# Sixteen attention steps take over the first conversion of the weights in an attention and Mish feed-forward kernel

## The chip, the cores and the metric

The kernel runs on one core of one Trainium2 chip. The metric is the device time of one execution in microseconds (us); the kernel before has a median of 900.63 us over three runs (898.88 to 900.71). A difference of 0.2%, about 1.8 us, is about what a measurement of this kernel can tell from no change.

## The reference

Attention with queries pooled in pairs (four batches, eight heads, 1152 keys of 64), and behind it a feed-forward layer with a Mish activation over 2304 rows of 512. All inputs are float32.

```python
q_pool = q.reshape(B, H, S // 2, 2, D).mean(axis=3)
scores = scale * np.matmul(q_pool, k.transpose(0, 1, 3, 2))
scores = scores - np.max(scores, axis=-1, keepdims=True)
attn = np.exp(scores)
attn = attn / (np.sum(attn, axis=-1, keepdims=True) + 1e-09)
attn_out = np.matmul(attn, v)
x = attn_out.transpose(0, 2, 1, 3).reshape(B * S_pooled, H * D)
h = x @ w_in
out = (h * np.tanh(np.log1p(np.exp(h)))) @ w_out
```

## The kernel before

The program has two parts. The first is attention in 32 **steps**: a pair of heads has two steps, one for each half of its queries. In a step the keys go by in nine chunks of 128. For chunk c of step i the kernel has these functions:

- `QK(i, c)` (L204, TensorE): four matrix products into a score tile `s` in PSUM. There are only two such tiles, so chunk c + 2 starts when chunk c's tile has been read.
- `CP(i, c)` (L214, ScalarE) copies the tile into `T3`, and `MX(i, c)` (L221, VectorE) takes it into the running maximum `rmax`, for c = 1 to 8. The two read one tile one after the other. "The sixth maximum" is `MX(i, 6)`, on the tile that the order of instructions calls `s_6`, and "the seventh" is `MX(i, 7)`.
- `MT`, `TMAX`, `MB` (L230 TensorE, L235 VectorE, L244 TensorE) turn the maxima into one per query, spread over all partitions as the tile `Mb`.
- `SUB` (L252, VectorE), `EXP` (L256, ScalarE), `PV` (L273, TensorE) subtract, exponentiate and multiply with the values, in four groups of chunks. `EXP` of group 1 comes ahead of that of group 0; `PV(i, 0)` waits for group 0.
- `ADD(i, 0)` to `ADD(i, 4)` (L262, L264, L266, GpSimd) sum the exponentials. `ADD(i, 0)` reads four chunks of `T3`, from SBUF, once group 0 is exponentiated. The next use of the same half of `T3`, `CP(i + 2, 0)`, waits for it.
- `QP` (L125, GpSimd) pools the queries of a coming pair, `TG` and `TGc` (L145, L148 TensorE; L156 to L161 ScalarE) transpose its keys and queries and copy them out of PSUM.

The second part is the feed-forward layer, on the weights split into a high and a low half. A 128-row piece of a weight matrix is made by `load_w(n)` (one or four DMAs on SyncE's queue) and six conversion stages `conv(n, 0)` to `conv(n, 5)`:

- stage 0: ScalarE, a scaled copy to the tile `wt` (L436);
- stages 1, 2 and 3: VectorE, all in int32 and 128x512: a shift of `wt` (L440), and two operations that take the raw weights and `wt` together, both from SBUF (L442, L446). Stage 3 also calls `load_w(n + 2)`;
- stage 4: ScalarE, the high half `wh` (L455);
- stage 5: GpSimd, the low half `wl`, `wt` minus `wh` (L458).

Pieces 0 to 3 are converted in the attention part, all others in the feed-forward part.

The order on every engine is written by hand. Each call has a due time in units of a step: `STEP` and `PAIR` give it relative to a step, so `(MX, 6, 0.245)` stands for i + 0.245 in step i. All calls are sorted by due time, and each engine runs its instructions strictly in that order. `CONV0` lists the due times of the six stages of pieces 0 to 3. Due time 4.245 is `MX(4, 6)`, 4.464 is `MX(4, 7)`, and 4.267 is `ADD(3, 0)`.

`first()` runs ahead of the sorted plan: it loads the first pair, keeps TensorE busy with 52 transposes that nothing reads, and prepares the first keys and queries.

Of the kernel before, what the change touches and what calls it, by code (L numbers as in the profile page):

```python
# [22 lines left out]
def tile_pooled_attention_then_mish_ffn(ctx: ExitStack, tc: tile.TileContext, q, k, v, moe_w_in, moe_w_out, out):  # L23
# [42 lines left out]
    if True:  # L66
# [22 lines left out]
        def load_q(p):  # L89
            if p >= B * NP:  # L90
                return
            b, hp = divmod(p, NP)
            qn = pre.tile([QB, 2, 6, P], F32, tag="qn", name=f"qn{p}")
            for j in range(2):
                sp.dma_start(out=qn[:, j], in_=q[b, 2 * hp + j].rearrange("(n p r) d -> p n (r d)", p=QB, r=2))
            raw[p] = [None, qn]

        def load_k(p):
            if p >= B * NP:
                return  # L100
            b, hp = divmod(p, NP)
            kn = pre.tile([P, NC, 2, D], F32, tag="kn", name=f"kn{p}")
            for j in range(2):
                o = kn[:, :, j] if p else T3[:, 1, j].rearrange("p a b -> p (a b)").rearrange("p (c d) -> p c d", d=D)
                sp.dma_start(out=o, in_=k[b, 2 * hp + j].rearrange("(p c) d -> p c d", c=NC))
                if p == 0:
                    (act.copy if j else dve.tensor_copy)(kn[:, :, j], o)
            raw[p][0] = kn
# [3 lines left out]
        def load_v(p):  # L112
            if p >= B * NP:
                return
            b, hp = divmod(p, NP)
            vs[p] = p2.tile([P, 2, NC, D], F32, tag="vn", name=f"vn{p}")
            sp.dma_start(out=vs[p], in_=v[b, 2 * hp:2 * hp + 2].rearrange("h (p c) d -> p h c d", c=NC))
# [3 lines left out]
        def QP(p):  # L121

            x = raw[p][1].rearrange("p j n m -> p n j m")
            qp = pre.tile([QB, 6, 2, D], F32, tag="qp", name=f"qp{p}")
            (pool if p else dve).tensor_tensor(qp, x[:, :, :, 0:D], x[:, :, :, D:2 * D], ALU.add)  # L125
            prepped[p] = qp.rearrange("p n j d -> p n (j d)")

        def qk_tiles(p):
            qT = pqk.tile([P, SQ], F32, tag="qT", name=f"qT{p}")
            kT = pqk.tile([P, NC, P], F32, tag="kT", name=f"kT{p}")  # L130
            qk[p] = (kT, qT)
# [3 lines left out]
        def kblock(p, c):  # L135
            return raw[p][0][:, c].rearrange("p j d -> p (j d)")
# [26 lines left out]
        def first():  # L163

            load_q(0)
            load_k(0)
            load_w(0)
            load_w(1)
            QP(0)
            if NWARM:  # L170
                x = ps1.tile([P, 4, P], F32R, tag="x", name="warm")
                for n in range(NWARM):
                    pe.transpose(x[:, n % 4], identr, identr)  # L173
            qk_tiles(0)
            kT, qT = qk[0]
            t = psS.tile([P, 2, 512], F32, tag="S", name="xq0")
            for n in range(6):
                pe.transpose(t[:, n // 3, n % 3 * QB:(n % 3 + 1) * QB], prepped[0][:, n], ident[0:QB, 0:QB])
            act.copy(qT[:, 0:HQ], t[:, 0, 0:HQ])
            dve.tensor_copy(qT[:, HQ:SQ], t[:, 1, 0:HQ])  # L180
            x = psS.tile([P, 8, P], F32, tag="S", name="xk0")
            for n in range(8):
                pe.transpose(x[:, n], kblock(0, n), ident)
            act.copy(kT[:, 0:4], x[:, 0:4])
            dve.tensor_copy(kT[:, 4:8], x[:, 4:8])
            x = ps1.tile([P, 512], F32, tag="x", name="xk0_2")
            pe.transpose(x[:, 0:P], kblock(0, 8), ident)
            act.copy(kT[:, 8], x[:, 0:P])
            load_q(1)
            load_k(1)  # L190

        rmaxs, Mbs, pvs, accs = {}, {}, {}, {}

# [222 lines left out]
        def load_w(n):  # L416
            if n >= len(pieces):
                return
            f, io = pieces[n]
            if io:  # L420
                r = wraw_p.tile([P, DM, 2], I32, tag="raw", name=f"ro{f}")
                sp.dma_start(out=r, in_=wo32[f * P:(f + 1) * P])
            else:
                r = wraw_p.tile([P, NKC, P, 2], I32, tag="raw", name=f"ri{f}")
                for c in range(NKC):
                    sp.dma_start(out=r[:, c], in_=wi32[:, c, f * P:(f + 1) * P])
                r = r.rearrange("p c m two -> p (c m) two")
            wraw[n] = r
# [90 lines left out]
        def O_(bu, f):  # L519
            gh, gl = gs.pop((bu, f))  # L520
            wh, wl = ws[f, 1]
            first, last = f in F0, f + 1 in F0
            if first:
                os_[bu] = o_tiles(bu)
            for t in range(UT // P):
                a, b = gh[:, t * P:(t + 1) * P], gl[:, t * P:(t + 1) * P]
                for m, (x, y) in enumerate(((a, wh), (a, wl), (b, wh))):
                    pe.matmul(os_[bu][t], x, y, start=(first and m == 0), stop=(last and m == 2))  # L528
# [67 lines left out]
            plan += [(i + t, fn, i, *a) for i in range(NS) if i < NS - 1 or fn not in GONE]  # L596
        plan += [(NS + t, fn, NS - 1) for fn, t in LAST.items()]
        for fn, *a, t in PAIR:
            first_p = 2 if fn in (load_q, load_k) else 0 if fn is load_v else 1
            plan += [(2 * p + t, fn, p, *a) for p in range(first_p, B * NP)]  # L600
        CONV0 = [
            (-0.26, -0.17, -0.16, -0.13, -0.05, -0.04),
            (-0.02, 0.07, 0.09, 0.10, 0.20, 0.21),
            (0.35, 0.40, 0.47, 0.49, 0.55, 0.56),
            (0.60, 0.66, 0.67, 0.78, 0.85, 0.86),
        ]
        for n, t in enumerate(CONV0):
            plan += [(t[m], conv, n, m) for m in range(6)]
# [4 lines left out]
        for g in range(len(seq) + 8):  # L613
            t = NS + T3F + DT * (g - 3)
            for fn, *a in FLOW:
                if fn in (split, convs):
                    plan.append((t, fn, g, *a))
                elif 0 <= g - a[0] < len(seq):
# [3 lines left out]
                    else:  # L622
                        plan.append((t, *e))
        first()
        plan.sort(key=lambda e: e[0])
        for _, fn, *a in plan:
# [32 lines left out]
```

## Time and profile before

| | us |
|---|---|
| median of three runs | 900.63 |
| the three runs | 900.71, 900.63, 898.88 |
| the profiled execution | 898.73 |
| its span in the profile | 897.0 |
| VectorE busy in the span | 591.7 |
| ScalarE busy in the span | 539.7 |
| GpSimd busy in the span | 454.8 |
| TensorE busy in the span, by modelled ends | 872.7 |

The span is the time from the first to the last instruction, 1.7 us less than the execution's time. A row of the timeline gives start, duration, engine, line, operation, result and operands, shapes, and in brackets the idle time of the engine ahead of it and what ended it. PE is TensorE's products, PEld its weight loads, DVE is VectorE, ACT ScalarE, POOL GpSimd. A row of the page's costliest groups gives the total busy time and the mean of one in ns. A row of busy time by stretches gives the stretch and its length, then the busy time (and instructions) of PE, PEld, DVE, ACT and POOL, then the granted clock as a share of full speed, the DMA share and GB/s.

### The profile page before, as it was taken

Reading aid. Unit: us, or ns where it says so; the run is one execution under the profiler, and the core shown is the slowest. Engines: PE = TensorE matmul, PEld = TensorE weight load, DVE = VectorE, ACT = ScalarE, POOL = GpSimd, SP = SyncE. Lnnn points to the kernel's source line nnn. Section 1 sums busy time; section 2 is a strip of 40 time slices with the busy share of each in tenths; the row PEclk is TensorE's granted clock in tenths of the full one; section 3 lists DMA queues with packets and bytes.
Section 4 is the critical chain, followed back from the end, with each engine's and each line's share of the span. In section 5 each row is a group of like instructions: output and inputs, shape, how many; then the busy total and the mean of one; then the engine's idle time right before and its main releaser. Section 6 shows DMA issues by size and latency. Waiting matters only on the chain.

```text
span 897.0 us, 14672 instructions
## 1 busy us (share of the span) xinstructions
PE 872.7 (97%) x5668; PEld 590.1 (66%) x5668; DVE 591.7 (66%) x812; ACT 539.7 (60%) x997; POOL 454.8 (51%) x268
## 2 busy tenths in 40 slices
PE   6899999999999999999998999999999999999997
PEld 4444444444444444444445899999999999999996
DVE  4898988998889888988897733443555334432222
ACT  4788888888888888888886753333333333322221
POOL 1489888988889888998889520111111011100000
PEclk9799999999999999999999999999999999999999
DMA  6412223132321323132200210111122011001112
GB/s 176 129 40 68 75 59 80 27 80 55 80 59 48 80 54 80 27 80 53 74 2 1 71 49 24 48 48 47 50 71 71 24 48 48 24 1 48 48 48 70
DMA packets 75109, 50.74 MB, mean 57 GB/s; under 512 B 37408, under 2 KB 68640, under 8 KB 75040
## 3 DMA queue, kind: packets, MB, share of 16 engines
q1 hardware_dynamic: 75040, 49.82, 19.8%
q8 instruction: 44, 0.72, 0.3%
q14 instruction: 25, 0.20, 0.1%
HBM read 45.09 MB, written 4.72 MB: 56 GB/s over the span
## 4 chain that ended last, share of the span: by engine, by line
PE 84%; ACT 7%; POOL 6%; DVE 2%; issue 1%; DVEq 0%; POOLq 0%; ACTq 0%
PE h L495 23%; PE s L204 16%; PE pv L273 13%; PE o L528 11%; POOL acc L262 5%; ACT T L214 3%; ACT T L256 3%; PE mt L230 2%; PE xt L145 2%; PE Mb L244 2%; PE xt L148 1%; DVE T L252 1%; PE Sb L295 1%; PE warm L173 1%; POOL xl L477 0%
## 5 line engine op out<-in xcount | busy, mean ns | idle before, releaser
L204 PE MATMUL s<-qT,kT 64*128 64x288 f32 x1152 | 211.9, 454 | 12.8 <-DVE rmax L221 6.3
L510 DVE TENSOR_TENSOR gl<-g,gh 128x256 fp32r<-128x256 f32 x144 | 66.3, 461 | 230.9 <-ACT gh L505 200.2
L500 ACT ACTIVATE g<-h 128x256 f32<-128x256 f32 x144 | 55.6, 386 | 249.2 <-PE h L495 249.1
L214 ACT COPY T<-s 128x576 f32<-128x576 f32 x288 | 181.4, 641 | 36.9 <-DVE rmax L221 16.1
L252 DVE TENSOR_TENSOR T<-T,Mb 128x1152 f32<-128x1152 f32 (+1 forms) x128 | 191.3, 1496 | 11.1 <-PE Mb L244 11.0
L273 PE MATMUL pv<-T,vn 128*64 128x288 f32 x1152 | 194.3, 428 | 1.2 <-ACT T L256 0.5
L221 DVE TENSOR_TENSOR rmax<-s,rmax 128x576 f32<-128x576 f32 x224 | 169.0, 754 | 37.3 <-ACT T L214 30.6
L458 POOL TENSOR_TENSOR wl<-wt,wh 128x512 fp32r<-128x512 f32 x32 | 41.8, 1308 | 256.2 <-ACT wh L455 212.3
L256 ACT ACTIVATE T<-T 128x1152 f32<-128x1152 f32 (+1 forms) x128 | 166.0, 1297 | 6.9 <-DVE T L252 4.9
L264 POOL TENSOR_TENSOR acc<-acc,T 128x1152 f32<-128x1152 f32 x64 | 168.7, 2636 | 2.7 <-ACT T L256 0.2
L204 PEld LDWEIGHTS s<-qT,kT 64*128 64x128 f32 x1152 | 89.5, 189 | 117.7 <-issue 40.8
L495 PE MATMUL h<-xh,wh 128*128 128x256 f32 x576 | 162.0, 281 | 0.0
L495 PE MATMUL h<-xh,wl 128*128 128x256 f32 x576 | 161.8, 281 | 0.0
L495 PE MATMUL h<-xl,wh 128*128 128x256 f32 x576 | 161.6, 281 | 0.0
L273 PEld LDWEIGHTS pv<-T,vn 128*64 128x64 f32 x1152 | 63.7, 136 | 88.6 <-issue 58.9
L495 PEld LDWEIGHTS h<-xh,wh 128*128 128x128 f32 x576 | 108.7, 189 | 8.1 <-issue 2.2
L495 PEld LDWEIGHTS h<-xl,wh 128*128 128x128 f32 x576 | 108.9, 189 | 6.0
L495 PEld LDWEIGHTS h<-xh,wl 128*128 128x128 f32 x576 | 109.2, 190 | 0.0
L262 POOL TENSOR_TENSOR acc<-T 128x1152 f32<-128x1152 f32 x32 | 84.7, 2645 | 44.6 <-ACT T L256 43.7
L528 PE MATMUL o<-wh,gh 128*128 128x512 f32 x146 | 57.7, 395 | 0.0
L528 PE MATMUL o<-wl,gh 128*128 128x512 f32 x146 | 57.5, 394 | 0.0
L528 PE MATMUL o<-wh,gl 128*128 128x512 f32 x146 | 57.3, 392 | 0.0
(380 smaller groups left out, 1094.2 us busy)
## 6 DMA issues: line engine op xcount, KB each, us to landing
qn<-in_q_dram SPq DMA_DIRECT2D x32, 288.0 KB, 3.8
vn<-in_v_dram SPq DMA_DIRECT2D x16, 576.0 KB, 4.9
kn<-in_k_dram SPq DMA_DIRECT2D x30, 288.0 KB, 4.1
ri<-in_moe_w_in_dram SPq DMA_DIRECT2D x64, 128.0 KB, 2.2
ro<-in_moe_w_out_dram SPq DMA_DIRECT2D x16, 512.0 KB, 3.5
out_dram<-xT SPq DMA_DIRECT2D x18, 256.0 KB, 2.6
T<-in_k_dram SPq DMA_DIRECT2D x2, 288.0 KB, 4.8
```

The lines of the kernel that those rows point to most:

```text
L204: pe.matmul(s[:, j, 0:HQ], kT[64 * j:64 * j + 64, c], qT[64 * j:64 * j + 64, hf * HQ:(hf + 1) * HQ], start=True, stop=True,)
L214: act.copy(T3[:, i % 2, c], ss[i, c])
L221: dve.tensor_tensor(r, ss[i, c], T3[:, i % 2, 0] if c == 1 else r, ALU.max)
L252: dve.tensor_tensor(x, x, Mbs[i][:, :, 0:HQ].unsqueeze(1).to_broadcast([P, w, 2, HQ]), ALU.subtract)
L256: act.activation(x, x, AF.Exp, scale=0.0625)
L262: pool.tensor_tensor(accs[i], t[:, 0:2], t[:, 2:4], ALU.add)
L264: pool.tensor_tensor(accs[i], accs[i], t[:, 2 * n + 2:2 * n + 4], ALU.add)
L273: pe.matmul(pvs[i][64 * j:64 * j + 64, 0:HQ], vn[:, j, c, :], T3[:, i % 2, c, j], start=(c == 0), stop=(c == NC - 1),)
L495: pe.matmul(h[:, 0:UT], a, b, start=(m == 0), stop=(m == len(seq) - 1))
L500: act.activation(g, hs[bu, f], AF.Mish)
L510: dve.tensor_tensor(gl, ch.pop((bu, f)), f32(gs[bu, f][0]), ALU.subtract)
L528: pe.matmul(os_[bu][t], x, y, start=(first and m == 0), stop=(last and m == 2))
```

## The change

`CONV0` is replaced. Before, the 24 stages have due times from -0.26 to 0.86, in the first step. Now stage m of piece n is due in step 4n + 2 and later: stage 0 at 4n + 2.73, the three VectorE stages at 4n + 3.30, 4n + 4.30 and 4n + 5.30, stage 4 at 4n + 5.73 and stage 5 at 4n + 6.955. The four pieces so reach from 2.73 to 18.955. In `first()` the loads of pieces 0 and 1 move behind the loads of the second pair, and the first load of the values, `load_v(0)`, moves ahead of them. The loads of pieces 2 and 3 hang on stage 3 of pieces 0 and 1 and go with them.

```diff
             load_q(0)
             load_k(0)
-            load_w(0)
-            load_w(1)
             QP(0)
...
             load_q(1)
             load_k(1)
+            load_v(0)
+            load_w(0)
+            load_w(1)
...
-            first_p = 2 if fn in (load_q, load_k) else 0 if fn is load_v else 1
+            first_p = 2 if fn in (load_q, load_k) else 1
...
         CONV0 = [
-            (-0.26, -0.17, -0.16, -0.13, -0.05, -0.04),
-            (-0.02, 0.07, 0.09, 0.10, 0.20, 0.21),
-            (0.35, 0.40, 0.47, 0.49, 0.55, 0.56),
-            (0.60, 0.66, 0.67, 0.78, 0.85, 0.86),
+            tuple(4 * n + 2 + a for a in (0.73, 1.30, 2.30, 3.30, 3.73, 4.955)) for n in range(4)
         ]
```

In the order of VectorE's instructions the first step looked so before (`rmax0` is step 0's maximum, `s0_4` its chunk 4; `wt0`, `wt1` and `ri0`, `ri1` belong to pieces 0 and 1):

```order
L221 TENSOR_TENSOR rmax0_216<-s0_3_223,rmax0_216 128x576
L440 TENSOR_SCALAR wt0_227<-wt0_227 128x512
L442 SCALAR_TENSOR_TENSOR wt0_227<-ri0_113,wt0_227 128x512
L221 TENSOR_TENSOR rmax0_216<-s0_4_230,rmax0_216 128x576
L446 SCALAR_TENSOR_TENSOR wt0_227<-ri0_113,wt0_227 128x512
L221 TENSOR_TENSOR rmax0_216<-s0_5_238,rmax0_216 128x576
L440 TENSOR_SCALAR wt1_250<-wt1_250 128x512
L442 SCALAR_TENSOR_TENSOR wt1_250<-ri1_118,wt1_250 128x512
L446 SCALAR_TENSOR_TENSOR wt1_250<-ri1_118,wt1_250 128x512
L221 TENSOR_TENSOR rmax0_216<-s0_6_253,rmax0_216 128x576
```

Of the change, the same place on VectorE (lines from 164 on are numbered a little differently):

```order
L222 TENSOR_TENSOR rmax0_218<-s0_3_225,rmax0_218 128x576
L222 TENSOR_TENSOR rmax0_218<-s0_4_230,rmax0_218 128x576
L222 TENSOR_TENSOR rmax0_218<-s0_5_236,rmax0_218 128x576
L222 TENSOR_TENSOR rmax0_218<-s0_6_242,rmax0_218 128x576
L222 TENSOR_TENSOR rmax0_218<-s0_7_247,rmax0_218 128x576
L222 TENSOR_TENSOR rmax0_218<-s0_8_257,rmax0_218 128x576
L222 TENSOR_TENSOR rmax1_268<-s1_1_262,T3_98 128x576
```

All conversion stages are gone from between the maxima of step 0, and from the same stretch of ScalarE and GpSimd.

Further on, step 4 on VectorE before, around its sixth and seventh maximum:

```order
L221 TENSOR_TENSOR rmax4_650<-s4_5_700,rmax4_650 128x576
L252 TENSOR_TENSOR T3_98<-T3_98,Mb3_684 128x1152
L221 TENSOR_TENSOR rmax4_650<-s4_6_712,rmax4_650 128x576
L221 TENSOR_TENSOR rmax4_650<-s4_7_725,rmax4_650 128x576
L252 TENSOR_TENSOR T3_98<-T3_98,Mb3_684 128x1728
L221 TENSOR_TENSOR rmax4_650<-s4_8_753,rmax4_650 128x576
```

The same place of VectorE in the change:

```order
L222 TENSOR_TENSOR rmax4_613<-s4_5_663,rmax4_613 128x576
L253 TENSOR_TENSOR T3_98<-T3_98,Mb3_647 128x1152
L222 TENSOR_TENSOR rmax4_613<-s4_6_675,rmax4_613 128x576
L443 SCALAR_TENSOR_TENSOR wt0_510<-ri0_201,wt0_510 128x512
L222 TENSOR_TENSOR rmax4_613<-s4_7_688,rmax4_613 128x576
L253 TENSOR_TENSOR T3_98<-T3_98,Mb3_647 128x1728
L222 TENSOR_TENSOR rmax4_613<-s4_8_717,rmax4_613 128x576
```

Stage 2 of piece 0 now stands between the two maxima of step 4. Stage 1 stands at the same place in step 3 and stage 3 in step 5; pieces 1, 2 and 3 follow four, eight and twelve steps later.

## Rows read from the trace of the kernel before

**Rows 1.** The page's costliest groups: the copy of a score tile, and stage 5.

```profile
L214 ACT COPY T<-s 128x576 f32<-128x576 f32 x288 | 181.4, 641 | 36.9 <-DVE rmax L221 16.1
...
L458 POOL TENSOR_TENSOR wl<-wt,wh 128x512 fp32r<-128x512 f32 x32 | 41.8, 1308 | 256.2 <-ACT wh L455 212.3
```

**Rows 2.** The chain that ended last, 90 to 130 us, shares by line.

```profile
by line: PE s L204 42.2%; PE pv L273 39.1%; PE xt L145 5.7%; PE mt L230 4.1%; PE Sb L295 3.6%; PE Mb L244 3.2%; PE xt L148 2.2%; issue 0.3%
```

**Rows 3.** Timeline of POOL: `ADD(i, 0)` of steps 0, 1, 4 and 5.

```profile
38.69 2.64 POOL L262 TENSOR_TENSOR acc<-T 128x1152 f32<-128x1152 f32 x1 [2.88 <-ACT T L256]
...
52.32 2.65 POOL L262 TENSOR_TENSOR acc<-T 128x1152 f32<-128x1152 f32 x1 [0.70 <-ACT T L256]
...
95.80 2.64 POOL L262 TENSOR_TENSOR acc<-T 128x1152 f32<-128x1152 f32 x1 [3.22 <-ACT T L256]
...
109.43 2.65 POOL L262 TENSOR_TENSOR acc<-T 128x1152 f32<-128x1152 f32 x1 [0.16 <-ACT T L256]
```

**Rows 4.** Timeline, step 0 from its fifth chunk to `PV(0, 0)`.

```profile
15.78 0.76 PE L204 MATMUL s<-qT,kT 64*128 64x288 f32 x4 [0.67 <-ACT T L214]
...
28.89 1.33 PE L230 MATMUL mt<-identr,rmax 128*128 128x128 f32 x5
...
31.91 0.80 PE L244 MATMUL Mb<-identr,m 128*128 128x128 f32 x6
...
33.84 0.62 ACT L455 CAST wh<-wt 128x512 fp32r<-128x512 f32 x1
...
34.81 1.19 ACT L256 ACTIVATE T<-T 128x1152 f32<-128x1152 f32 x1
...
38.67 1.19 PE L273 MATMUL pv<-T,vn 128*64 128x288 f32 x8 [0.54 <-ACT T L256]
```

**Rows 5.** Busy time and granted clock (PEclk) of three stretches of the start.

```profile
14.40:17.80 3.40, 2.15 (x12) 0.86 (x12) 3.04 (x5) 1.77 (x4) 0.64 (x1) 1.00 0.06 12
17.80:21.20 3.40, 0.83 (x6) 0.30 (x4) 1.73 (x3) 2.14 (x4) 1.27 (x1) 1.00 0.42 154
21.20:31.40 10.20, 7.39 (x25) 3.62 (x25) 8.41 (x14) 5.37 (x9) 2.55 (x2) 0.50 0.56 167
```

**Rows 6.** Timeline, step 6: `MX(6, 7)`, and the weight loads of `QK(6, 8)`.

```profile
110.55 0.76 DVE L221 TENSOR_TENSOR rmax<-s,rmax 128x576 f32<-128x576 f32 x1 [0.29 <-ACT T L214]
...
111.36 0.30 PEld L204 LDWEIGHTS s<-qT,kT 64*128 64x128 f32 x4 [0.23 <-DVE rmax L221]
```

**Rows 7.** Timeline: `MX(5, 6)`, `MX(5, 7)`, `CP(6, 0)` and `CP(5, 8)`, `TGc` of queries.

```profile
94.91 0.75 DVE L221 TENSOR_TENSOR rmax<-s,rmax 128x576 f32<-128x576 f32 x1
...
96.92 0.76 DVE L221 TENSOR_TENSOR rmax<-s,rmax 128x576 f32<-128x576 f32 x1 [1.25 <-ACT T L214]
...
98.47 1.18 ACT L214 COPY T<-s 128x576 f32<-128x576 f32 x2 [0.19 <-POOL acc L262]
...
103.71 0.40 ACT L161 COPY qT<-xt 128x288 f32<-128x288 f32 x1 [0.90 <-PE xt L148]
```

**Rows 8.** Timeline, VectorE and GpSimd together on operands in SBUF.

```profile
488.77 2.63 POOL L264 TENSOR_TENSOR acc<-acc,T 128x1152 f32<-128x1152 f32 x1
...
489.31 2.37 DVE L510 TENSOR_TENSOR gl<-g,gh 128x256 fp32r<-128x256 f32 x1 [3.61 <-ACT gh L505]
...
494.50 1.81 POOL L477 TENSOR_TENSOR xl<-xT,xh 128x256 fp32r<-128x256 f32 x2
...
495.74 1.11 DVE L442 SCALAR_TENSOR_TENSOR wt<-ri,wt 128x512 int32<-128x512 int32 x1
...
499.99 0.69 DVE L442 SCALAR_TENSOR_TENSOR wt<-ro,wt 128x512 int32<-128x512 int32 x1
...
499.99 1.29 POOL L477 TENSOR_TENSOR xl<-xT,xh 128x256 fp32r<-128x256 f32 x1 [3.68 <-ACT xh L476]
...
506.98 0.42 DVE L440 TENSOR_SCALAR wt<-wt 128x512 int32<-128x512 int32 x1
...
293.19 0.73 POOL L477 TENSOR_TENSOR xl<-xT,xh 128x256 fp32r<-128x256 f32 x1 [0.77 <-ACT xh L476]
```

## The prediction

> **What bounds the kernel now.** I read the chain that ended last first. In the attention steps it runs on TensorE alone: products of scores and values, transposes, 0.3% for anything else [rows 2]. VectorE, ScalarE and GpSimd have idle time there, but only where the row of the one behind it is not a product: whatever makes a score product start later lengthens the step. Next I read where the steps settle. `ADD(0, 0)` and `ADD(1, 0)` start 13.63 us apart, and so do those of steps 4 and 5 [rows 3]. So the attention part keeps its pace from `PV(0, 0)`, at 38.67 [rows 4], and all ahead of it is a ramp. The change does two things: it shortens the ramp, and it puts work between two maxima of twelve steps that run at TensorE's pace. The end is the ramp's gain against what those twelve steps lose.
>
> **The ramp.** In step 0 a score tile goes through product (0.76), copy (0.64) and maximum (0.76), one after the other, and the tile two chunks on waits for the maximum [rows 1, 4, 6]. A hand-over takes 0.05: `MX(6, 7)` ends at 110.55 + 0.76 = 111.31 and the weights that waited for it are loaded at 111.36 [rows 6]. One link is so 0.76 + 0.64 + 0.76 + 3 x 0.05 = 2.31. `QK(0, 5)` starts at 15.78 [rows 4], which is ahead of any place where a conversion stage has cost something. From it three links, chunks 5, 7 and 8 (chunk 6 and the next step's first chunk go by in between), end `MX(0, 8)` at 15.78 + 6.93 = 22.71. `MT` stands behind one more product, 0.05 + 0.76 later: 23.5. Before, it starts at 28.89 [rows 4]: **5.4** gained.
>
> From `MT` to `MB` it took 3.02 (28.89 to 31.91), and `MT` 1.33 of it, at a granted clock of 0.50, the lower level of 1.2 GHz; `MB` already ran at full clock, 0.80 for six transposes [rows 4, 5]. At full clock `MT` takes about half, 0.6 less, and the score product and four key transposes between the two are also cut; a third VectorE stage of about 0.7 stood in the way as well. I take **1.1**, with 0 (the clock falls as before) and 1.5 as bounds. From `MB` to `EXP` of group 1 ScalarE did a `wh` of 0.62 first [rows 4], and the copies behind it had their data: **0.5**. From there to `PV(0, 0)`, 3.86, nothing is taken out. In sum 7.0: `PV(0, 0)` at 31.7. Bounds 5.4 and 7.5.
>
> The fall of the clock came behind a stretch with 0.83 of 3.40 us busy on TensorE; the stretch ahead of that had 2.15, and no fall behind it [rows 5]. In the new ramp the stretch from 17.8 to 21.2 holds three score products of 0.76, about 2.3 us. I therefore expect no fall.
>
> The moved loads cost nothing: keys and queries of the first pair stand ahead of the weights in the queue before and after, and the weights have until step 2. What covers the later loads is a step or more: `load_w(2)` now stands in SyncE's queue ahead of `load_k(4)` and waits for stage 3 in step 5, but those keys are transposed more than a step later. If that cover were gone, each of two such waits would cost the few microseconds of one landing.
>
> **The steps: ScalarE and GpSimd.** Stage 4 (0.62) goes ahead of a copy of queries that waits 0.90 for TensorE [rows 4, 7]; stage 0, of the same size, stands in the other kind of step ahead of the copy of keys, which waits for the same engine. Both go at nothing. Stage 5 (1.31 [rows 1]) stands between the last addition of an odd step and `ADD` of the even one, where GpSimd waits 3.22 [rows 3]: nothing. Without those waits each would cost its own length, four times.
>
> **The steps: VectorE.** Between the two maxima VectorE idles 1.25 us in odd steps [rows 7] and 0.29 in even ones [rows 6]. Stages 1 (0.42) and 3 (0.69, of one form with stage 2) [rows 8] fall on odd steps, 3, 5, 7 and so on; stage 2 on the even steps 4, 8, 12 and 16. By length alone, stage 2 would be late by 0.4. But there is GpSimd. Rows 8 hold the case: `gl`, two inputs in SBUF, usually 0.4, began at 489.31 inside an addition of GpSimd and ended at 491.68, 0.28 after that addition (491.40). Stage 2 itself, started at 495.74 inside a run of GpSimd that ended at 496.31, took 1.11 and ended 0.54 after it. All of VectorE's work in the attention steps has one input in PSUM; stages 2 and 3 are the first there with two in SBUF.
>
> In an even step `MX(6, 6)` ends at 110.26 (0.29 ahead of `MX(6, 7)`), and `ADD(5, 0)` runs from 109.43 to 112.08 [rows 3, 6]. Stage 2, due at 110.26, can only end at 112.08 + 0.54 = 112.62. `MX(6, 7)` starts then and not at 110.55: about 2.0 later. Behind it on VectorE are the last `SUB` and `MX(6, 8)`; `QK(6, 8)` waits for exactly this maximum, 0.05 behind its end [rows 6], and all of TensorE's queue behind that. The two products that follow wait for maxima of the same chain, so nothing is made up. Four times 2.0 is **8.0**. Bounds: 1.6 if GpSimd does not hold it (0.4 each), 8.4 if it also waits out the next start.
>
> In odd steps the order is the other way. `MX(5, 6)` ends at 95.66, the stage can go at once, and `ADD(4, 0)` starts at 95.80 [rows 3, 7]. VectorE is first by about 0.15. Then GpSimd waits: at 499.99 both started together, VectorE took its usual 0.69 and GpSimd's operation 1.29 where it takes 0.73 alone [rows 8]; it was held 0.56, up to 0.13 before VectorE's end. Stage 3 from 95.66 to 96.35 holds `ADD(4, 0)` until 96.2, 0.4 late; stage 1, to 96.08, until 95.95, 0.15 late. `CP(6, 0)` waits for that addition [rows 7], and the score product of the next chunk for that copy. Four times 0.55 is **2.2**; bounds 0 and 3.
>
> The Trainium skill has a rule here, "SBUF — State Buffer", section "Who interferes with whom": VectorE and GpSimd share one pair of ports, a VectorE instruction with two SBUF inputs, or in a mode that uses both ports, takes part in it against a GpSimd instruction that reads SBUF, and whoever issues first has the pair for the whole instruction. By that, stages 3 and 1 would hold GpSimd to their own end, 0.13 longer each, and the term would be 3.2 in place of 2.2. By the row it lets go earlier, and I keep the row.
>
> **Sum.** -7.0 + 8.0 + 2.2 = +3.2; where GpSimd's additions have a little slack this shrinks, to some +2.5, which I take. Durations are from the profiled execution, 898.73 us, which lies 1.9 below the median of 900.63; of the four known times two are near 898.8 and two near 900.7. From their middle, 899.7, I get **902.2 us**. The likeliest case's own range is 900.5 to 904.5.
>
> **Rivals.**
> 1. *The additions do not hold stage 2.* It would be late by 0.4 only, and odd steps cost nothing: -7.0 + 1.6 = -5.4, 894.3 us. For it: the rows that show a hold are from the feed-forward part, with other tiles. Against: one is this very operation, another this very addition. It decides as soon as stage 2 takes 0.7 in step 4. Chance 0.14.
> 2. *GpSimd wins in odd steps too.* The lead is 0.15 us. If `ADD(4, 0)` starts first, stage 3 ends at 98.44 + 0.54, `MX(5, 7)` starts at 99.0 and not at 96.92, 2.1 late in place of 0.4: +6.8 for four, 909 us; with stage 1 as well about 915. For it: the margin is thin and the steps are disturbed. Against: it is the same in every odd step, and both sides shift with TensorE. Chance 0.10.
> 3. *The clock falls in the new ramp too.* Then 1.1 of the gain is lost and some products more: +1.5, 903.7 us. For it: TensorE is only two thirds busy there. Chance 0.12.
> 4. *The waits are partly made up*, because TensorE has slack that the modelled ends of products hide, or the ramp gains 7.5: within 1.8 of no change, about 900 us. Chance 0.16.
>
> The forecast itself has 0.48, and about a quarter of it lies below +0.2%. The range 897.0 to 907.5 leaves out rival 1 and most of rival 2. A measurement tells 0.2%, 1.8 us, from no change: faster 0.15, same 0.27, slower 0.58.
>
> **What would show it.** `PV(0, 0)` near 31.7; no stretch at the lower clock before 40 us; stage 2 with about 2.4 us in steps 4, 8, 12 and 16, ending 0.54 behind an `ADD`, and `MX(i, 7)` right behind it; `ADD(i, 0)` of even steps 4, 8 and so on 0.4 longer than 2.64; each group of four steps from 2 to 18 longer by 2.5, all others unchanged. Wrong would be a stage 2 of 0.7, a stage 3 of 3 us, a `PV(0, 0)` above 34, or an attention part in which the stalls are there and the steps are not longer.

## The result: 0.6% slower, twice the forecast loss

| | before | changed |
|---|---|---|
| median, us | 900.44 | 905.51 |
| lowest and highest of six runs | 898.88, 901.07 | 903.33, 907.62 |
| profiled execution | 898.73 | 904.78 |
| its span | 897.0 | 903.0 |

The ratio is 1.0059, with a 95% interval of 1.0045 to 1.0073. The sign was right and the time lies inside the forecast's range, but outside the likeliest case's own range of 900.5 to 904.5: +2.5 us was forecast, the medians differ by 5.1 and the two profiled executions by 6.05.

The timeline of the changed kernel, first the places of [rows 4], then one step of each kind. Line 441 is stage 1, 443 stage 2, 447 stage 3, 222 `MX`, 263 `ADD(i, 0)`:

```profile
15.40 0.76 PE L205 MATMUL s<-qT,kT 64*128 64x288 f32 x4 [0.67 <-ACT T L215]
...
22.95 0.77 PE L231 MATMUL mt<-identr,rmax 128*128 128x128 f32 x5
...
24.83 0.80 PE L245 MATMUL Mb<-identr,m 128*128 128x128 f32 x6
...
27.20 1.19 ACT L257 ACTIVATE T<-T 128x1152 f32<-128x1152 f32 x1
...
31.06 1.19 PE L274 MATMUL pv<-T,vn 128*64 128x288 f32 x8 [0.54 <-ACT T L257]
...
31.09 2.65 POOL L263 TENSOR_TENSOR acc<-T 128x1152 f32<-128x1152 f32 x1 [16.54 <-ACT T L257]
...
59.44 0.42 DVE L441 TENSOR_SCALAR wt<-wt 128x512 int32<-128x512 int32 x1
...
59.65 2.70 POOL L263 TENSOR_TENSOR acc<-T 128x1152 f32<-128x1152 f32 x1 [3.22 <-ACT T L257]
...
73.34 2.63 POOL L263 TENSOR_TENSOR acc<-T 128x1152 f32<-128x1152 f32 x1 [0.16 <-ACT T L257]
...
74.09 2.43 DVE L443 SCALAR_TENSOR_TENSOR wt<-ri,wt 128x512 int32<-128x512 int32 x1
...
77.24 0.76 PE L205 MATMUL s<-qT,kT 64*128 64x288 f32 x4 [1.75 <-DVE rmax L222]
...
91.43 0.68 DVE L447 SCALAR_TENSOR_TENSOR wt<-ri,wt 128x512 int32<-128x512 int32 x1
...
91.64 2.97 POOL L263 TENSOR_TENSOR acc<-T 128x1152 f32<-128x1152 f32 x1 [5.17 <-ACT T L257]
...
105.60 2.65 POOL L263 TENSOR_TENSOR acc<-T 128x1152 f32<-128x1152 f32 x1 [0.15 <-ACT T L257]
```

Read it as a balance of `ADD` starts against [rows 3]. `ADD(0, 0)` starts 7.60 earlier than before (38.69, now 31.09), `ADD(4, 0)` only 4.16 earlier (95.80, 91.64), `ADD(5, 0)` 3.83 earlier (109.43, 105.60). Between the first two lie one stage 1 and one stage 2, which took 3.44 of the gain; stage 3 took 0.33 more. Stage 2 starts inside `ADD(3, 0)` and ends 0.55 behind it (73.34 + 2.63 = 75.97; 74.09 + 2.43 = 76.52).

The chain that ended last, over the same place (start, length, what). "issue" behind stage 2 is time in which VectorE waits for nothing that the profile shows, inside its own instruction:

```profile
73.42 0.75 DVE rmax L222
74.17 0.06 DVE wt L443
74.23 2.21 issue
76.44 0.76 DVE rmax L222
77.20 0.04 issue
77.24 0.76 PE s L205 x4
78.00 1.07 PE pv L274 x4
79.07 1.26 PE s L205 x4
80.33 1.16 PE pv L274 x4
81.49 0.70 PE s L205 x4
```

The chain leaves TensorE exactly where the prediction put it: sixth maximum, stage 2, seventh maximum, score product. But then something follows that the prediction does not have. The three products behind the one that waited take 1.07 to 1.26, where the next takes 0.70 again. The stretches around this place (the first two), behind it in step 8, around it in step 12 (two) and behind it in step 16 show why (PE, PEld, DVE, ACT, POOL busy, granted clock, DMA share, GB/s):

```profile
74.70:78.10 3.40, 1.66 (x12) 0.77 (x12) 3.40 (x3) 1.81 (x4) 3.40 (x3) 0.99 0.58 149
78.10:81.50 3.40, 3.40 (x14) 0.92 (x12) 2.74 (x4) 2.56 (x3) 2.30 (x2) 0.50 0.00 0
...
139.50:142.90 3.40, 3.40 (x14) 1.23 (x12) 2.23 (x4) 2.33 (x3) 2.29 (x2) 0.50 0.00 0
...
196.40:199.80 3.40, 1.65 (x12) 0.66 (x11) 3.40 (x3) 1.87 (x3) 3.40 (x3) 1.00 0.68 156
199.80:203.20 3.40, 3.40 (x25) 1.59 (x25) 3.40 (x6) 2.81 (x3) 2.30 (x2) 1.00 0.00 0
...
259.00:262.40 3.40, 3.40 (x14) 1.09 (x12) 2.62 (x4) 2.28 (x2) 2.30 (x2) 0.50 0.00 0
```

Right behind the idle gap of 1.75 us on TensorE the granted clock was 0.50, the lower level of 1.2 GHz, from 78.07 to 81.48. The same happened in steps 8 and 16 and not in step 12, though TensorE was as busy ahead of it (1.66 and 1.65). Worked out for every step from the starts of `ADD(i, 0)`, in both profiles: the four stage 1 cost 0.06 each, the four stage 2 3.38, 3.43, 1.84 and 3.38, the four stage 3 0.33 or 0.34 each, every other step of the attention part at most 0.03, but for 0.28 in the last one. In sum -7.60 + 0.24 + 12.03 + 1.33 + 0.28 = +6.28, the difference of the spans (6.0) within 0.3.

### The profile page after: what moved, and what is told of

Same layout as the page of the kernel before. It is cut to its first block, busy times and chain, and to the rows that moved or that the text cites. A ratio compares the mean times of both kernels' runs of the same rounds, so it can differ in the third digit from the quotient of the medians.

```text
span 903.0 us, 14673 instructions
## 1 busy us (share of the span) xinstructions
PE 874.2 (97%) x5668; PEld 589.5 (65%) x5668; DVE 598.3 (66%) x812; ACT 540.4 (60%) x997; POOL 457.9 (51%) x268
## 4 chain that ended last, share of the span: by engine, by line
PE 80%; ACT 7%; POOL 7%; issue 3%; DVE 3%; DVEq 0%; POOLq 0%; ACTq 0%
PE h L496 22%; PE s L205 15%; PE o L529 11%; PE pv L274 11%; POOL acc L263 5%; ACT T L215 4%; ACT T L257 3%; PE mt L231 2%; PE xt L145 2%; PE Mb L245 2%; DVE rmax L222 2%; PE xt L148 1%; DVE T L253 1%; PE warm L171 1%; PE Sb L296 1%
## 5 line engine op out<-in xcount | busy, mean ns | idle before, releaser
L274 PE MATMUL pv<-T,vn 128*64 128x288 f32 x1152 | 196.4, 432 | 1.0 <-ACT T L257 0.5
```

The source lines that it names most:

```text
L274: pe.matmul(pvs[i][64 * j:64 * j + 64, 0:HQ], vn[:, j, c, :], T3[:, i % 2, c, j], start=(c == 0), stop=(c == NC - 1),)
```

## The experiments

The theory now: stage 2 is held by GpSimd's addition, which costs 1.85 us a step, and the clock that falls behind the stall costs 1.55 more in three steps of four. Its rivals: something else in the twelve steps costs the time (ScalarE's or GpSimd's stages, or mere VectorE length), or the 3.4 us are one long consequence of the stall.

**All three VectorE stages in odd steps** (`e1_all_odd`), where VectorE comes ahead of the addition:

```diff
-            tuple(4 * n + 2 + a for a in (0.73, 1.30, 2.30, 3.30, 3.73, 4.955)) for n in range(4)
+            tuple(6 * n + 2 + a for a in (0.73, 1.30, 3.30, 5.30, 5.73, 6.955)) for n in range(4)
```

> The changed kernel with all three VectorE stages in odd steps, where VectorE starts ahead of GpSimd's first addition (a piece every six steps, so that each odd step holds one stage). If what is lost is the hold of stage 2 by GpSimd and the fall of the clock behind it: no maximum later than in the kernel before, stages of 0.42 and 0.68, steps longer by 0.06 (stage 1) and 0.33 (stages 2 and 3), no stretch at the lower clock in the steps, -7.6 + 4 x 0.72 = -4.7, about 894 us against 898.7 to 900.6 of before. If the loss is the work itself, anywhere between two maxima: as the changed kernel, about 905 us.

Measured: median 894.85 (894.52 to 898.02, seven runs), ratio 0.9956 (0.9944 to 0.9969). Its timeline at stage 2 of piece 0:

```profile
88.38 0.68 DVE L443 SCALAR_TENSOR_TENSOR wt<-ri,wt 128x512 int32<-128x512 int32 x1
88.59 2.97 POOL L263 TENSOR_TENSOR acc<-T 128x1152 f32<-128x1152 f32 x1 [3.21 <-ACT T L257]
89.72 0.76 DVE L222 TENSOR_TENSOR rmax<-s,rmax 128x576 f32<-128x576 f32 x1 [0.65 <-ACT T L215]
```

The same operation that took 2.43 takes 0.68, because it starts 0.21 ahead of the addition and not 0.75 behind its start. Now GpSimd is the one held: 2.97 in place of 2.65. Stage 2 costs 0.33 a step, like stage 3, and in the profile the clock does not fall in any of these steps (granted clock 1.00 from 37 to 300 us). With the same stages and none of them in an even step the kernel is faster than before: what makes the change a loss hangs on the even steps.

**No VectorE stage in the attention part** (`e2_no_dve`):

```diff
-            if m == 1:
+            if n < 4 and m < 4:
+                if m == 3 and n < 2:
+                    load_w(n + 2)
+            elif m == 1:
```

> The changed kernel without the three VectorE stages of pieces 0 to 3, so that these weights are not converted rightly; the ScalarE and GpSimd stages and all loads stay. It measures the ramp alone. If ScalarE's and GpSimd's stages are hidden: -7.6, about 891 us, every step as long as before. If they cost something in the steps, it shows here in the steps that hold them, and the time lies above 892.

Measured: 893.26 (890.34 to 897.09, six runs), ratio 0.9939 (0.9916 to 0.9962). In its profile (an execution of 891.79) the first addition starts 7.14 earlier than before, and every step is within 0.03 of before's, but for 0.17 in the last one. The median lies above 892, which was to be the sign of a cost in the steps; the steps show none, and the slower runs are those with a lower mean clock (0.999 in the run of 890.34, 0.988 in that of 897.09). So stages 0, 4 and 5 and the moved loads cost nothing in these steps, and all that is lost in them is lost through VectorE.

**Stage 2 alone left out** (`e3_no_stage2`), one run:

```diff
+            if n < 4 and m == 2:
+                return
```

> The changed kernel without stage 2 of pieces 0 to 3 alone (its weights are then wrong); stages 1 and 3 stay. If stage 2 carries the loss: 0.06 and 0.33 in the steps with stages 1 and 3, -7.6 + 1.6 = -6.0, about 893 us, no fall of the clock in the steps. If the odd steps carry more than that, above 895.

Measured: 897.62. The steps came out as the theory says, 0.07 for stage 1, 0.34 for stage 3, nothing in the steps where stage 2 was. The time did not, and by itself it would have spoken for the other answer (above 895): in this run the clock was 0.50 in the ramp, from 17.46 to 27.70 and again from 34.53 to 37.94: the ramp gained only 4.27, and step 1 lost 1.16. That is rival 3 of the prediction, seen for the first time, and it costs more than the 1.5 us that I had put on it.

**Stage 2 with one input** (`e4_one_input`), at its old place in even steps:

```diff
+            if n < 4 and m == 2:
+                y = p1.tile([P, 1], F32, tag="y", name=f"y{n}")
+                dve.tensor_reduce(y, wt[n], axis=AX.X, op=ALU.max)
+                return
```

> The changed kernel with stage 2 of pieces 0 to 3 replaced by a reduction of the same 512 elements to one, with one input in SBUF, at the same place in even steps (these weights are then wrong). If two inputs in SBUF beside GpSimd's addition make the hold: the reduction takes about 0.7, the seventh maximum is 0.25 to 0.4 late, no fall of the clock, -7.6 + 1.6 + 1.6 at most, 893 to 895 us. If it is VectorE work at this place whatever it reads: a hold of 2.4 and about 905 us.

Measured: 893.71 (893.56 to 894.79, four runs), ratio 0.9939 (0.9924 to 0.9954). Its timeline in step 4:

```profile
73.45 2.66 POOL L263 TENSOR_TENSOR acc<-T 128x1152 f32<-128x1152 f32 x1 [0.16 <-ACT T L257]
...
74.20 0.67 DVE L442 TENSOR_REDUCE y<-wt 128x1 f32<-128x512 f32 x1
74.80 0.74 DVE L222 TENSOR_TENSOR rmax<-s,rmax 128x576 f32<-128x576 f32 x1
```

A reduction of nearly stage 2's own length (0.67 against 0.68), inside the same addition, is not held, and the step loses 0.07 or 0.08. VectorE's length is not the cause; the hold is. The reduction differs from stage 2 in more than the number of its inputs: it reads f32 and writes only 128x1. So the run shows that this form is free and does not by itself say which operand matters. Nor does one input alone make an operation free: stage 1 has one, and holds the addition 0.06. The Trainium skill, "SBUF — State Buffer", section "Who interferes with whom", says that it is the second input from SBUF, and that a reduction never takes part. The trace agrees as far as the reduction goes: 0.67, where stage 2 took 2.43.

**TensorE kept busy through the stall** (`e5_keep_pe_busy`): the changed kernel, with twelve transposes that nothing reads put behind the first score product of the next step, into columns of that tile that are not used, in the four steps where stage 2 stands:

```diff
+            if c == 0 and i in (5, 9, 13, 17):
+                for _ in range(12):
+                    pe.transpose(s[:, 0, 320:320 + P], ident, ident)
```

> The changed kernel with twelve transposes that nothing reads on TensorE in each of steps 4, 8, 12 and 16, between the products of the next step's first chunk and of the ninth chunk, where TensorE otherwise idles 1.75 us. They write columns of the score tile that hold no scores. If the part of the loss above 1.85 a step is the fall of the clock behind that idle time: no stretch at the lower clock in the steps, each of the four steps longer by 1.85 alone, three times 1.55 less than the changed kernel, about 900 us. If it is something else of the hold: as the changed kernel, 905 us, or more by the transposes.

Measured: 901.63 (899.03 to 905.88, ten runs), ratio 1.0024 (1.001 to 1.0039). Timeline and stretches at step 4; line 215 is the added transposes, 446 stage 2, 205 the score product that waits:

```profile
74.34 2.44 DVE L446 SCALAR_TENSOR_TENSOR wt<-ri,wt 128x512 int32<-128x512 int32 x1
...
75.68 1.53 PE L215 MATMUL s<-identr 128*128 128x128 f32 x12
...
77.50 0.76 PE L205 MATMUL s<-qT,kT 64*128 64x288 f32 x4 [0.29 <-DVE rmax L225]
...
78.19 0.71 PE L277 MATMUL pv<-T,vn 128*64 128x288 f32 x4
```

```profile
75.00:78.40 3.40, 3.11 (x24) 2.09 (x24) 3.40 (x3) 1.80 (x4) 3.40 (x3) 1.00 0.64 155
78.40:81.80 3.40, 3.40 (x23) 1.53 (x21) 3.40 (x6) 2.78 (x4) 2.31 (x2) 1.00 0.03 5
```

Stage 2 takes 2.44 as in the changed kernel and the score product waits for the same maximum, but the clock stays at 1.00 and the products behind take 0.71. Each of the four steps now costs 1.84 or 1.85. That parts the 3.38: 1.85 are the stall, 1.53 the clock behind it. It also explains step 12 of the changed kernel, which lost 1.84 without any added work: there the clock did not fall. The median is above the expected 900, and the ten runs scatter: the profiled one, 900.67, has a mean clock of 0.997, the four above 903 have 0.988 to 0.992. Where the clock fell in those, no rows show.

**The stages ahead of the sixth maximum** (`e6_before_sixth`), in odd steps and before the addition has started:

```diff
-            tuple(4 * n + 2 + a for a in (0.73, 1.30, 2.30, 3.30, 3.73, 4.955)) for n in range(4)
+            tuple(6 * n + 2 + a for a in (0.73, 1.20, 3.20, 5.20, 5.73, 6.955)) for n in range(4)
```

> All three VectorE stages in odd steps, ahead of the sixth maximum and not behind it; there GpSimd waits, and the seventh maximum waits for ScalarE 1.25 us longer than the sixth takes. If the 0.33 of an odd step comes from holding GpSimd's first addition: no step longer at all, ramp gain alone, about 891 us in the undisturbed profile, 0.991 of before. If VectorE work in an odd step costs by its length: 0.3 to 0.7 a stage, 895 us or more.

Measured: 895.15 (890.0 to 895.86, six runs), ratio 0.9937 (0.9919 to 0.9954). Timeline at stage 2, and the ramp's stretches:

```profile
91.50 0.69 DVE L443 SCALAR_TENSOR_TENSOR wt<-ri,wt 128x512 int32<-128x512 int32 x1
92.11 0.75 DVE L222 TENSOR_TENSOR rmax<-s,rmax 128x576 f32<-128x576 f32 x1
92.39 2.65 POOL L263 TENSOR_TENSOR acc<-T 128x1152 f32<-128x1152 f32 x1 [3.22 <-ACT T L257]
```

```profile
12.20:15.60 3.40, 1.80 (x12) 0.66 (x10) 1.85 (x3) 2.02 (x4) 1.81 (x1) 1.00 1.26 262
15.60:29.30 13.70, 12.74 (x44) 6.48 (x45) 6.79 (x9) 5.20 (x9) 0.00 (x0) 0.50 0.48 132
```

The steps lose nothing, at most 0.04 each: stage 2 is over when the addition starts, which keeps its 2.65. The time was to be about 891 and came out where the other answer had it (895 or more), but not for that answer's reason: in this profile the clock fell in the ramp for 13.7 us, and the ramp gained 3.41 and not 7.1 to 7.6. The run of 890.0 had a mean clock of 0.999 over its span, the other five 0.989 to 0.994, the profiled one among them; that the clock fell in the ramp of the other four too is likely and not shown.

**The same with TensorE kept busy in the ramp** (`e7_ramp_pe_busy`): as the last one, and three transposes that nothing reads behind each score product of step 0 but the first:

```diff
+            if i == 0 and c > 0:
+                x = ps1.tile([P, 4, P], F32R, tag="pv", name=f"busy{c}")
+                for n in range(3):
+                    pe.transpose(x[:, n], identr, identr)
```

> The kernel with the stages ahead of the sixth maximum, and three transposes that nothing reads behind each score product of step 0 but the first, so that TensorE idles less in the ramp. If the runs some 3 us above the rest come from a fall of the clock in the ramp, as one profile showed it (17.5 to 27.7 us): no such runs, all within 1.5 us, median at the low end of the kernel without the transposes, about 890.5. If the scatter comes from elsewhere: the same scatter, and 0 to 1 us more for the transposes.

Measured: **891.56** (891.27 to 892.8, four runs), ratio 0.9909 (0.9896 to 0.9921), the lowest median of all; it was to be about 890.5, and the runs span 1.53. Stretches of its ramp:

```profile
14.40:17.80 3.40, 3.11 (x21) 1.64 (x20) 1.83 (x3) 2.05 (x4) 0.07 (x1) 1.00 1.05 351
17.80:21.20 3.40, 3.01 (x22) 1.53 (x20) 1.51 (x2) 1.96 (x4) 0.00 (x0) 1.00 0.87 237
21.20:24.60 3.40, 2.94 (x19) 1.54 (x19) 2.81 (x4) 1.60 (x3) 0.00 (x0) 1.00 0.24 45
```

TensorE has 2.9 to 3.1 of 3.4 us busy, the clock stays at its upper level of 2.4 GHz, and the ramp gains 7.46. One profile and four runs (mean clock 0.995 to 0.998) are few: `e4_one_input`, without these transposes, also had four runs at 0.995 to 0.997. It is against `e6_before_sixth`, with five of six at 0.994 or less, that they make a difference. This version is what the change could have been: the ramp's gain, nothing lost in the steps, 0.9% below the kernel before.

**Stage 3 behind the seventh maximum** (`e8_behind_add`), one run: as `e6_before_sixth`, with stage 3 at 5.47, so that it falls into the addition in odd steps too. It forces the order of rival 2 of the prediction, GpSimd first, on stage 3:

```diff
-            tuple(4 * n + 2 + a for a in (0.73, 1.30, 2.30, 3.30, 3.73, 4.955)) for n in range(4)
+            tuple(6 * n + 2 + a for a in (0.73, 1.20, 3.20, 5.47, 5.73, 6.955)) for n in range(4)
```

> The kernel with the stages ahead of the sixth maximum, but stage 3 behind the seventh maximum of its odd step, inside GpSimd's first addition. If whoever starts first decides: stage 3 takes about 1.4, ends 0.54 behind the addition, and the last subtraction starts 1.3 later, so four steps are longer by 1.2 to 1.4, with a further 1.5 where the clock falls: 896 to 902 us. If even and odd steps differ for another reason: stage 3 takes 0.7 and costs at most that.

Measured: 899.37, with the clock at 0.50 in the ramp from 15.57 to 29.22 (the ramp gained 3.48). Timeline at stage 3 of piece 0:

```profile
120.84 2.64 POOL L263 TENSOR_TENSOR acc<-T 128x1152 f32<-128x1152 f32 x1 [3.24 <-ACT T L257]
...
122.64 1.40 DVE L447 SCALAR_TENSOR_TENSOR wt<-ri,wt 128x512 int32<-128x512 int32 x1
```

Stage 3 starts inside the addition, which ends at 123.48, and ends 0.56 behind it, at 124.04, in 1.40 us. So the hold does not belong to stage 2 or to even steps, but to whoever starts second. The four steps lost 1.08, 1.07, 0.88 and 0.79, about 0.3 less on average than the 1.2 to 1.4 expected; why is open. The time lies in the expected range by luck: the ramp's fall, some 4 us, put it there, and without it the estimate is about 895.5, below the range.

**The old ramp with TensorE kept busy** (`e9_before_pe_busy`): the kernel before, with eight unread transposes behind each score product of step 0 but the first. It was to tell how much of before's ramp was its clock, and how much the conversion stages.

```diff
+            if i == 0 and c > 0:
+                x = ps1.tile([P, 4, P], F32R, tag="pv", name=f"busy{c}")
+                for n in range(8):
+                    pe.transpose(x[:, n % 4], identr, identr)
```

> The kernel before, with eight transposes that nothing reads behind each score product of step 0 but the first, to part the ramp's 7.6 us into stages and clock. If the part between the transposed maxima and the first exponentials (2.2 us) is mostly the lower clock from 21.2 to 31.4 us: no such stretch, the first addition 1 to 2 us earlier than in the kernel before, about 897.5 us. If the stages alone made the ramp long: the first addition at 38.7 as before, within 0.3 us, whatever the clock.

Measured: 899.59 (898.22 to 900.83, ten runs), ratio 1.0 (0.9991 to 1.001). The clock was low all the same, from 25.18 to 32.00, and the first addition started 0.81 later. The experiment failed to keep the clock up, so it does not tell the two apart.

## Why the prediction was half right

**What bounds the kernel, and the ramp: right.** From `QK(0, 5)` to `MT` it took 7.55 us (forecast 7.7), from `MT` to `MB` 1.88 (1.9), from there to `EXP` 2.37 (2.4), and on to `PV(0, 0)` 3.86 (3.86): a gain of 7.2 for the forecast 7.0. `PV(0, 0)` came at 31.06, not 31.7; 0.4 of this is that the keys came sooner in that run (`QK(0, 5)` at 15.40, before 15.78), and with it the gain of 7.6 lies just above the stated bound of 7.5 (whose own terms add up to 7.4). ScalarE's and GpSimd's stages and the loads cost nothing in the steps, as forecast (`e2_no_dve`).

**Odd steps: right, a little smaller.** VectorE won the race each time, stage 3 held the addition 0.33 (forecast 0.4) and stage 1 0.06 (0.15). The steps lost just that, 1.6 us for the four pairs, forecast 2.2. The Trainium skill, "SBUF — State Buffer", section "Who interferes with whom", says that the holder keeps the pair of ports for the whole instruction; by that the estimate was 3.2. The trace differs: GpSimd goes on about 0.14 before VectorE's end (stage 3 ends at 91.43 + 0.68 = 92.11, the addition was held 0.33, to 91.97), as the row at 499.99 in [rows 8] had shown with 0.13.

**Even steps: the mechanism right, the size wrong.** Stage 2 was held until 0.55 behind the addition's end (forecast 0.54) and took 2.43 (about 2.4), `MX(i, 7)` came right behind it, and TensorE had to wait. The step that failed is "Four times 2.0 is **8.0**". The stall itself was a little smaller than forecast, 1.85 each and 7.4 for four. But in three of the four steps the clock fell behind the stall, at 1.55 each, and the term measured 12.0. I had asked only of the ramp whether the clock would fall, from [rows 5], and not of the idle gap of some 2 us that I was myself putting into TensorE four times. With the gap filled and the clock held up (`e5_keep_pe_busy`), what is left of the change costs 1.5 us at the median and 1.9 in the profiled execution, near the +2.5 that the sum without the clock came to. The time lies inside the range 897.0 to 907.5 because that was wide, not for a reason that the prediction gives.

**"GpSimd's additions have a little slack": wrong.** The shrink of the sum from +3.2 to +2.5 rested on no row. No step gave anything back, so rival 4 did not occur either.

**Rivals 1 and 2** fell: stage 2 was held at every one of its places, and VectorE was first in every odd step. An operation that is not held takes another form (`e4_one_input`), and GpSimd is first at another place (`e8_behind_add`).

**Rival 3**, the clock in the new ramp, did not occur in the profile of the changed kernel, but it was priced too low. Among the eight profiles of kernels with the new ramp and no added transposes in it, the clock fell in the ramp in three (`e3_no_stage2`, `e6_before_sixth`, `e8_behind_add`), and there the ramp gained 3.4 to 4.3 and not 7.1 to 7.6: some 3 to 4 us, not 1.5. That would also account for much of the spread of the changed kernel, 903.33 to 907.62, where the fastest run had a mean clock of 0.993 and the slowest 0.985; those runs have no rows, so this is inferred, and another number of falls behind the stalls, at 1.55 each, would do it as well.

**What stays open.** What decides in which runs the clock falls in the ramp, and why step 12 was spared: the busy time of the stretch ahead does not tell them apart. From 12.20 to 15.60 `e4_one_input` had 1.79 of 3.40 us and no fall, `e6_before_sixth` 1.80 and a fall; at the stalls it was 1.66 with a fall and 1.65 without. And how before's slow ramp divides between its stages and its clock: `e9_before_pe_busy` does not tell, but `e3_no_stage2` gives an estimate. Its ramp is free of stages and was at the lower clock for 10.2 us, as long as before's (21.2 to 31.4), and gained 4.27. So some 4 us of the gain are the stages, and the other 3 of the 7.1 to 7.6 the clock; the two stretches do not lie over the same products, so this is rough.

## What to carry to other kernels

When work is put between two steps of the engine that sets the pace, ask two questions of the profile: whether an instruction of another engine that is running at that moment will hold it up, and what TensorE's clock does behind the gap that the wait leaves. Here moving the three VectorE stages to places where they are over when GpSimd's addition starts, and not inside it, turned a loss of 0.6% into a gain of 0.6%, and a few transposes that nothing reads, put where TensorE waits anyway, brought that to 0.9% (four runs). Price a stall with the slower products behind it, not with its length alone.

## What was not expected of the hardware

- One idle gap of 1.75 us on TensorE, between stretches in which it is full, was followed in three steps of four by 3.41 us at the lower clock; this cost 1.55 us, nearly as much as the stall (1.85).
- In a ramp where TensorE is half to three quarters busy, the clock fell in three profiles of eight, for 10.2 to 13.7 us. With three unread transposes behind each product it did not fall in the profile, and four runs lay within 1.6 us.
- A held VectorE instruction of this form (128x512, two inputs in SBUF) ended 0.54 to 0.56 behind the addition's end whatever was left of the addition when it started: in 2.43 us where 1.88 of it was left, in 1.40 where 0.84 was. GpSimd's next operation was held in its turn: the scaling of `pvs` behind `ADD(3, 0)` took 1.24 in place of some 0.81.
